# Linear attention beside a gated FFN on one core: Q and K weights loaded in row chunks among the first x tiles, and another order of phase 1

## The chip, the cores and the metric

The kernel runs on one core of a Trainium2 chip. A core has a matrix engine (TensorE, PE in the profile), three engines for elementwise work (VectorE or DVE, ScalarE or ACT, GpSimd or POOL), a queue engine (SyncE or SP) and 16 DMA engines. Each engine works through its own list of instructions in order; engines wait for each other and for transfers by semaphores. Data lies in SBUF (128 partitions); TensorE writes to PSUM, which has eight banks of 128 x 512 float32. The metric is device time in microseconds.

## The reference

With x of 2048 rows and 512 columns in bfloat16, the result is x plus a linear attention block plus a gated FFN, both on the layer norm of x. The attention has 32 heads of 16 columns.

```python
xn = _layernorm(x, axis=-1)
# attention
q, k, v = ...            # xn @ wqkv, split and put by heads
phi = lambda t: jnp.where(t > 0, t + 1, jnp.exp(t)) + 1e-6
pq, pk = phi(q), phi(k)
kv = jnp.einsum("bhsd,bhse->bhde", pk, v)
z = jnp.einsum("bhsd->bhd", pk)
num = jnp.einsum("bhqd,bhde->bhqe", pq, kv)
den = jnp.einsum("bhqd,bhd->bhq", pq, z)[..., None] + 1e-6
A = (num / den) @ wo
# FFN
B = (_silu(xn @ w_gate) * (xn @ w_up)) @ w_down
out = x + A + B
```

## The kernel before

The 2048 rows are 16 tiles of 128; the 512 columns are four chunks of 128. The program lists every operation with the tiles it reads and writes (`K.add`), and a small planner puts in the semaphore waits that these need. The order in the list is the order on each engine.

Phase 1 takes each row tile t through: statistics of the layer norm (step S, VectorE: bn_stats and bn_aggr), 1/std by a logarithm and an exponent on ACT (R), the normalised tile xn on VectorE (L), POOL (P) or ACT (N, then A), its transpose by a DMA (D, issued by SP) or on TensorE (W, X, with the eviction w, Z), the projections K and Q (K and k, Q and q: two halves of four matmuls of 512 columns), phi on them (exponent on ACT: x for K, y for Q; minimum on POOL: m, n; sum on VectorE: s, u), and G += xn^T pk, four matmuls into banks 0 to 3 over all tiles (step G). K and Q go round banks 4 to 7: `nextbank()` hands them out in turn, and the sum (s, u) frees them. For five tiles Q is copied off its bank by ACT (z), and its sum is made much later from the copy.

Tiles 0 and 1 are special (`CENTRED`): they are transposed on TensorE after the mean alone is taken off (a, b: two column halves on VectorE; c, d: two transposes each; e on ACT and f on VectorE evict them into `xcT`), and the 1/std enters later, as the scale of the exponent; r, o, j, J make the other factors. Tile 1's mean comes from ACT (M), and C centres it.

The order of phase 1 is written out by hand: the text given to `run()` is a list of steps, a letter and a tile each. SP issues the x loads ahead of it (tiles 0, 1, 3 to 15; ACT issues half of tile 0 and tile 2), then the transposing loads D in the order of the text, and behind them the weights of gate and up, V, wo and down. Wq and Wk are four loads of two row chunks each, two on ACT and two on SP, behind x tile 3. `keep_busy` runs matmuls on a constant into bank 7: NWARM of them at the start, and step F two of 256 columns.

Phase 2 has 56 groups gu(j) of four gate and four up matmuls, two banks each (4, 5 for even j, 6, 7 for odd j), with a SiLU on ACT and a product on VectorE (`hop`). From the G of phase 1 come GT (evicted ahead of j = 0) and kv (in j = 2). The sum of pk over all rows is made in two halves: POOL adds tiles 0 to 9 behind its last step of phase 1 (`z_add(0, i)`), VectorE the others between products; `z_bf` (behind hop(6)) adds the halves, and the denominators come from it by way of DMAs from j = 13 on. Row tiles of the result are made from j = 19 on.

Lines that matter: 207 to 227 the loads, 251 the warm-up, 257 to 302 statistics and centring, 354 to 368 transposes and evictions, 381 to 397 banks and projections, 399 to 432 phi, 470 to 499 the steps and their order, 500 to 509 the later weights, 515 to 537 gate and up, 558 z_bf, 637 on the order of phase 2.

## Time and profile before

| | us |
|---|---|
| median of 3 runs | 213.74 (212.69 to 214.31) |
| span of the profiled execution | 211.5 |
| busy: TensorE | 207.4 |
| busy: VectorE | 133.9 |
| busy: ACT | 69.6 |
| busy: POOL | 65.4 |

The span runs from the first to the last instruction of one profiled execution; the time of a run also has what lies around it. Busy time is the union of an engine's instructions, so TensorE at 98% says that it nearly always has something in hand, not that this is all necessary work: the warm-up counts too. The page cuts the span into 40 slices of 5.3 us, and each digit is a tenth of busy time:

```profile
PE   8999999999999999999999999999999999999996
...
DVE  3999988964765369746546585756647754625122
ACT  5698977406363333031221322130123131220000
POOL 3697877899500162202102021202202210000000
DMA  5933442399921201111011011011010111011101
```

Phase 1 is the first nine slices: there VectorE, ACT and POOL are nearly as busy as TensorE. Behind it they have room. DMA is busy at the start (x, Wq, Wk) and around the end of phase 1 (the other weights). The rest of a page has the chain of waits that ended last, groups of instructions with their mean duration, and transfers from issue to landing.

### The profile page before, as it was taken

The page shows a single profiled execution, that of the slowest core. Times are in us where ns is not written, and L with a number is a line of the kernel's source. Part 1 is how long each engine was busy: PE and PEld are TensorE (multiplying, and loading weights), DVE is VectorE, ACT ScalarE, POOL GpSimd, SP SyncE. Part 2 cuts the span into 40 slices and gives each one's busy share as a digit, 9 for nine tenths or more (in the row PEclk, how much of TensorE's full clock was granted, in tenths as well). Part 3 has the DMA queues.
Part 4 walks back from the last instruction along what each step waited for, and adds up shares of the span by engine and source line. Part 5 has one row for each costly group of instructions (what it writes and reads, how often), then busy time and mean ns, then how long its engine had stood idle before and what let it go on. Part 6 is the DMA issues. An engine that isn't in the chain of part 4 may idle for free.

```text
span 211.5 us, 2716 instructions
## 1 busy us (share of the span) xinstructions
PE 207.4 (98%) x991; PEld 96.2 (45%) x1010; DVE 133.9 (63%) x228; ACT 69.6 (33%) x144; POOL 65.4 (31%) x89
## 2 busy tenths in 40 slices
PE   8999999999999999999999999999999999999996
PEld 3344444444544444444444444444444444444455
DVE  3999988964765369746546585756647754625122
ACT  5698977406363333031221322130123131220000
POOL 3697877899500162202102021202202210000000
DMA  5933442399921201111011011011010111011101
GB/s 179 355 86 76 79 95 56 88 385 371 356 68 25 53 0 25 25 50 50 2 50 25 25 29 50 0 50 25 28 50 0 26 50 50 4 49 25 50 25 53
DMA packets 28285, 16.30 MB, mean 77 GB/s; under 512 B 18032, under 2 KB 28144, under 8 KB 28272
## 3 DMA queue, kind: packets, MB, share of 16 engines
q1 hardware_dynamic: 27440, 15.41, 26.1%
q10 hardware_dynamic: 832, 0.72, 1.0%
q8 instruction: 8, 0.13, 0.3%
q14 instruction: 5, 0.04, 0.1%
HBM read 9.96 MB, written 2.10 MB: 57 GB/s over the span
## 4 chain that ended last, share of the span: by engine, by line
PE 94%; DMA 2%; DVE 1%; issue 1%; SPq 1%; POOL 0%; ACT 0%; DVEq 0%
PE pb L522 45%; PE pb L620 23%; PE pb L391 12%; PE pb L616 7%; PE pb L440 6%; DMA wqkv<-in_A_wqkv_dram 2%; SPq L181 1%; PE pb L547 0%; PE pb L610 0%; DVE pq L430 0%; DVE hT L535 0%; POOL ef L419 0%; ACT ef L412 0%; PE pb L358 0%; DVE xn L328 0%
## 5 line engine op out<-in xcount | busy, mean ns | idle before, releaser
L530 ACT ACTIVATE sil<-pb 128x512 bf16<-128x512 f32 x56 | 33.3, 597 | 102.4 <-PE pb L522 98.7
L535 DVE TENSOR_TENSOR hT<-pb,sil 128x512 bf16<-128x512 f32 x56 | 38.2, 689 | 42.8 <-PE pb L522 39.9
L522 PE MATMUL pb<-xnT,wg 128*128 128x512 bf16 x224 | 57.8, 379 | 0.4
L522 PE MATMUL pb<-xnT,wu 128*128 128x512 bf16 x215 | 56.0, 379 | 0.2
L580 POOL TENSOR_TENSOR pz<-pq,zbc 128x512 f32<-128x512 bf16 x16 | 22.2, 1392 | 96.8 <-DVE den L587 79.5
L620 PE MATMUL pb<-wd,hT 128*128 128x512 bf16 (+2 forms) x247 | 50.8, 355 | 0.2
L620 PEld LDWEIGHTS pb<-wd,hT 128*128 128x128 bf16 x252 | 23.6, 98 | 24.9
L522 PEld LDWEIGHTS pb<-xnT,wu 128*128 128x128 bf16 x224 | 21.8, 98 | 26.4 <-DVE hT L535 1.4
L522 PEld LDWEIGHTS pb<-xnT,wg 128*128 128x128 bf16 x224 | 21.9, 98 | 25.8
L626 DVE TENSOR_TENSOR out_sb<-pb,x_sb 128x512 bf16<-128x512 f32 (+2 forms) x18 | 11.4, 633 | 23.1 <-PE pb L620 22.1
L391 PE MATMUL pb<-wqkv,xnT 128*128 128x512 bf16 x110 | 25.1, 379 | 0.2
L599 DVE TENSOR_TENSOR pq<-pq,rden 128x512 bf16<-128x512 bf16 x16 | 20.6, 1290 | 0.6
L419 POOL TENSOR_SCALAR ef<-ef 128x512 bf16<-128x512 bf16 x25 | 15.6, 622 | 5.7 <-ACT ef L412 5.4
L391 PEld LDWEIGHTS pb<-wqkv,xnT 128*128 128x128 bf16 x112 | 10.9, 98 | 13.3 <-DVE pk L430 0.4
L616 PE MATMUL pb<-M,pk 128*128 128x512 bf16 (+2 forms) x71 | 16.7, 355 | 0.2
L412 ACT ACTIVATE ef<-pb 128x512 bf16<-128x512 f32 x25 | 14.8, 593 | 3.9 <-PE pb L391 3.9
L258 DVE BATCH_NORM_STATS2 stats<-x_sb 128x6 f32<-128x512 bf16 x16 | 10.8, 678 | 3.2 <-DMA x_sb<-in_A_x_dram 3.2
L440 PE MATMUL pb<-pk,xn 128*128 128x512 bf16 x55 | 12.5, 379 | 0.1
L587 DVE TENSOR_REDUCE den<-pz 128x32 f32<-128x512 f32 x16 | 10.8, 675 | 0.0
L616 PEld LDWEIGHTS pb<-M,pk 128*128 128x128 bf16 x72 | 6.8, 98 | 7.4
L463 POOL TENSOR_TENSOR zacc<-zacc,pk 128x512 f32<-128x512 f32 x8 | 9.9, 1242 | 0.6
L430 DVE SCALAR_TENSOR_TENSOR pk<-pb,ef 128x512 bf16<-128x512 f32 x14 | 9.5, 683 | 0.6 <-POOL ef L419 0.3
(74 smaller groups left out, 111.1 us busy)
## 6 DMA issues: line engine op xcount, KB each, us to landing
out_dram<-out_sb SPq DMA_DIRECT2D x15, 128.0 KB, 1.9
x_sb<-in_A_x_dram SPq DMA_DIRECT2D x14, 128.0 KB, 4.6
wg<-in_B_w_gate_dram SPq DMA_DIRECT2D x2, 896.0 KB, 8.2
wu<-in_B_w_up_dram SPq DMA_DIRECT2D x2, 896.0 KB, 9.6
wd<-in_B_w_down_dram SPq DMA_DIRECT2D x2, 896.0 KB, 13.0
wqkv<-in_A_wqkv_dram ACTq DMA_DIRECT2D x2, 256.0 KB, 4.7
wqkv<-in_A_wqkv_dram SPq DMA_DIRECT2D x2, 256.0 KB, 5.4
wqkv<-in_A_wqkv_dram SPq DMA_DIRECT2D x1, 512.0 KB, 8.9
```

Of the source, the lines that this page charges most:

```text
L391: K.add("pe", [(lambda e, c=c: e.matmul(banks[b][:, :], src[:, c, t * P:(t + 1) * P], wqkv[:, c, col:col + D], start=(c == 0), stop=(c == ...
L412: K.add("act", lambda e: e.activation(buf, banks[b][:, :], ACT.Exp), r=[B(b)], w=[bkey])
L419: K.add("pool", lambda e: e.tensor_scalar(out=buf, in0=buf, scalar1=top, scalar2=0.0, op0=ALU.min, op1=ALU.max), r=[bkey] + tkeys, w=[bkey])
L440: K.add("pe", [(lambda e, c=c: e.matmul(banks[c][:, :], src[:, t, c * P:(c + 1) * P], pk[:, t, :], start=first, stop=last)) for c in range ...
L522: fns.append(lambda e, c=c, b=b, w_=w_: e.matmul(banks[b][:, :], w_[:, c, fc * P:(fc + 1) * P], xnT[:, c, C * 512:(C + 1) * 512], start=(c ...
L530: K.add("act", lambda e: e.activation(sil[:, j % 2, :], banks[gb(j)][:, :], ACT.Silu), r=[B(gb(j))], w=[("sil", j % 2)])
L535: K.add("dve", lambda e: e.tensor_tensor(out=hT[:, C % 2, fc, :], in0=banks[gb(j) + 1][:, :], in1=sil[:, j % 2, :], op=ALU.mult), r=[B(gb( ...
L580: K.add("pool", lambda e: e.tensor_tensor(out=pz[:, t % 2, :].rearrange("q (g p) -> q g p", g=NG), in0=pq[:, t, :].rearrange("q (g p) -> q ...
L599: K.add("dve", lambda e: e.tensor_tensor(out=heads(pq[:, t, :]), in0=heads(pq[:, t, :]), in1=rden[:, i, :][:, :, None].broadcast_to([P, NH ...
L616: fns = [(lambda e, g=g: e.matmul(banks[bank][:, 0:hi - lo], pk[:, t, g * P:(g + 1) * P], M[:, g, lo:hi], start=(g == 0), stop=False)) for ...
L620: fns = [(lambda e, fc=fc: e.matmul(banks[bank][:, 0:hi - lo], hT[:, C % 2, fc, jj * P:(jj + 1) * P], wd[:, fc, lo:hi], start=False, stop= ...
L626: K.add("dve", lambda e: e.tensor_tensor(out=out_sb[:, t % 2, lo:hi], in0=banks[bank][:, 0:hi - lo], in1=x_sb[:, t, lo:hi], op=ALU.add), r ...
```

## The change

Wq and Wk are loaded in four row chunks of 128 rows each, K on SP and Q on ACT, and x tiles 0, 1 and 2 in column halves on both queues among them; ACT also loads tile 3. The other x tiles become steps of the order (l), issued by SP between the transposing loads. The statistics of tile 0 are taken from two halves. Tile 1 is centred like tile 0 (a, b from VectorE's statistics, with transposes c, d and evictions g, h of its own); M, C, N and A are no longer used. A projection step names its chunks: `K0:0` is chunk 0 of K of tile 0, `Q2:01` two chunks, `K3` all four; a bank's first and last chunk set start and stop. K and Q of tile 2 use banks 0 and 1, and phi gets two more buffers for them. The order of phase 1 is new. Of the warm-up, seven matmuls of 512 columns and two of 256 stay, all at the start.

```diff
-SPLIT = (0, 1, 2, 3)
-NWARM = 8
+NC = len(CENTRED)
+NH2 = 3
+LOWBANK = {(1, 2): 0, (0, 2): 1}
+NWARM = 7
...
-        ef = sb("ef", [P, 4, D], bf)
+        ef = sb("ef", [P, 6, D], bf)
...
-        def wpart(eng, i, h):
-            load(eng, ("wqkv", i, h), wqkv[:, 2 * h:2 * h + 2, i * D:(i + 1) * D],
-                 A_wqkv[2 * h * P:(2 * h + 2) * P, i * D:(i + 1) * D].rearrange("(c p) f -> p c f", p=P))
-
-        xhalf("sp", 0, 0)
-        xhalf("act", 0, 1)
-        xload("sp", 1)
-        xload("act", 2)
-        xload("sp", 3)
-        wpart("act", 1, 0)
-        wpart("sp", 1, 1)
-        wpart("act", 0, 0)
-        wpart("sp", 0, 1)
-        for t in range(4, 16):
-            xload("sp", t)
+        def wchunk(eng, i, c):
+            load(eng, ("wqk", i, c), wqkv[:, c, i * D:(i + 1) * D], A_wqkv[c * P:(c + 1) * P, i * D:(i + 1) * D])
+
+        for eng, h in (("sp", 0), ("act", 1)):
+            xhalf(eng, 0, h)
+            wchunk(eng, 1 - h, 0)
+            xhalf(eng, 1, h)
+            wchunk(eng, 1 - h, 1)
+            xhalf(eng, 2, h)
+            wchunk(eng, 1 - h, 2)
+            wchunk(eng, 1 - h, 3)
+            if h:
+                xload(eng, 3)
...


         def xk(t):
-            return [("x", 0, 0), ("x", 0, 1)] if t == 0 else [("x", t)]
+            return [("x", t, 0), ("x", t, 1)] if t < NH2 else [("x", t)]

         def bn1(t):
             K.add("dve", lambda e: e.bn_stats(stats[:, t, :], x_sb[:, t, :]), r=xk(t), w=[("st", t)])

+        def bnhalf(h):
+            K.add("dve", lambda e: e.bn_stats(stats[:, h * NT, :], x_sb[:, 0, h * H:(h + 1) * H]), r=[("x", 0, h)], w=[("st", h * NT)])
+
         def bn2(t):
             K.add("dve", lambda e: e.bn_aggr(mv[:, t, :], stats[:, t, :]), r=[("st", t)], w=[("mv", t)])
+
+        def stat0():
+            bnhalf(0)
+            bnhalf(1)
+            K.add("dve", lambda e: e.bn_aggr(mv[:, 0, :], stats[:, 0::NT, :]), r=[("st", 0), ("st", NT)], w=[("mv", 0)])

         def rs(t):
             sl = slice(t, t + 1)
...

         ring = [0]
         at = {}
+        begun = {}

         def nextbank():
             ring[0] += 1
             return 4 + (ring[0] - 1) % 4

-        def proj(col, i, t, halves=(0, 1)):
-            if 0 in halves:
-                at[i, t] = nextbank()
-            b = at[i, t]
+        def proj(i, t, cs):
+            if (i, t) not in at:
+                at[i, t] = LOWBANK[i, t] if (i, t) in LOWBANK else nextbank()
+                begun[i, t] = 0
+            b, col = at[i, t], i * D
             src = xcT if t in CENTRED else xnT
-            for h in halves:
-                K.add("pe", [(lambda e, c=c: e.matmul(
-                    banks[b][:, :], src[:, c, t * P:(t + 1) * P], wqkv[:, c, col:col + D],
-                    start=(c == 0), stop=(c == NDC - 1))) for c in (2 * h, 2 * h + 1)],
-                    r=([("xcT", t, h)] if t in CENTRED else xkeys(t)) + [("wqkv", i, h)], w=[B(b)])
-
-        def rest(t):
-            return (1,) if t in SPLIT else (0, 1)
+            fns = []
+            for c in cs:
+                first, last = begun[i, t] == 0, begun[i, t] == NDC - 1
+                begun[i, t] += 1
+                fns.append(lambda e, c=c, first=first, last=last: e.matmul(
+                    banks[b][:, :], src[:, c, t * P:(t + 1) * P], wqkv[:, c, col:col + D], start=first, stop=last))
+            keys = sorted({("xcT", t, c // 2) for c in cs}) if t in CENTRED else xkeys(t)
+            K.add("pe", fns, r=keys + [("wqk", i, c) for c in cs], w=[B(b)])
+
+        def efslot(b):
+            return b - 4 if b >= 4 else b + 4

         def phi_keep(t):
             b, slot = at[0, t], later[t]
...
                   r=[fkey, ("pk", t)], w=[key])

         def stat(t):
+            if t == 0:
+                stat0()
+                return
             bn1(t)
             bn2(t)

...
-            "c": lambda t: transp(t, 0, 0, 2), "d": lambda t: transp(t, 1, 2, 4),
-            "e": lambda t: evac(t, 0, "act", 0, 2), "g": lambda t: evac(t, 0, "dve", 0, 2),
-            "h": lambda t: evac(t, 1, "act", 2, 4), "f": lambda t: evac(t, 1, "dve", 2, 4),
+            "c": lambda t: transp(t, 2 * t, 0, 2), "d": lambda t: transp(t, 2 * t + 1, 2, 4),
+            "e": lambda t: evac(t, 2 * t, "act", 0, 2), "g": lambda t: evac(t, 2 * t, "dve", 0, 2),
+            "h": lambda t: evac(t, 2 * t + 1, "act", 2, 4), "f": lambda t: evac(t, 2 * t + 1, "dve", 2, 4),
-            "K": lambda t: proj(D, 1, t, (0,)), "k": lambda t: proj(D, 1, t, rest(t)), "x": lambda t: phi_exp(1, t), "m": lambda t: phi_min(1, t), "s": lambda t: phi_sum(1, t),
-            "Q": lambda t: proj(0, 0, t, (0,)), "q": lambda t: proj(0, 0, t, rest(t)), "y": lambda t: phi_exp(0, t), "z": phi_keep, "n": lambda t: phi_min(0, t), "u": lambda t: phi_sum(0, t), "G": gacc, "F": lambda t: keep_busy(t, 256),
+            "l": lambda t: xload("sp", t), "K": lambda t, cs=range(NDC): proj(1, t, cs), "x": lambda t: phi_exp(1, t), "m": lambda t: phi_min(1, t), "s": lambda t: phi_sum(1, t),
+            "Q": lambda t, cs=range(NDC): proj(0, t, cs), "y": lambda t: phi_exp(0, t), "z": phi_keep, "n": lambda t: phi_min(0, t), "u": lambda t: phi_sum(0, t), "G": gacc, "F": lambda t: keep_busy(t, 256),
+            words = [(w[0], int(w[1:].split(":")[0]), [int(c) for c in w.split(":")[1]] if ":" in w else None)
+                     for w in text.split()]
+            late = {t for k, t, _ in words if k == "z"}
+            later.update({t: i for i, t in enumerate(t for k, t, _ in words if k == "u" and t in late)})
+            for k, t, cs in words:
+                steps[k](t) if cs is None else steps[k](t, cs)
...
         run("""
...
+            F1 l4 l8 F1 S0 l12 b0 d0 R0 a0 c0 e0 r0 Q0:0 S1 a1 c1 Q0:1 J0 b1 d1 R1 r1 o1 l11 f0 S2 h1 o0 g1 K0:0 K0:1
+            l13 K0:2 l14 Q0:2 Q1:0 Q1:1 R2 K0:3 K1:0 L2 W2 Q0:3 K1:1 K1:2 K1:3 l9 x0 Q1:2 m0 z0 S3 R3 w2 y0 S4 P3 R4
+            P4 Q2:01 K2:01 K2:23 x2 m2 S8 X3 x1 l10 Z3 s0 Q2:23 s2 D4 m1 s1 Q1:3 K3 l6 J1 S10 y2 z2 R8 x3 S12 S14 P8
+            m3 z1 Q3 L0 l15 z3 y1 R12 P12 G2 G0 y3 s3 R14 P14 G1 S9 K4 x4 Q4 l7 m4 s4 G3 y4 S13 R10 S6 D8 n4 u4 n3 Q8
+            y8 z8 D12 P10 l5 K8 D14 x8 G4 R9 L9 R6 K12 x12 m8 s8 S7 D10 D9 R13 Q12 P6 Q14 y14 m12 L13 n1 s12 y12 K14
+            x14 G8 G12 S15 n14 u14 Q9 R7 n12 u12 K9 D13 m14 L1 K10 L7 y9 x9 m9 n9 D6 s14 x10 K6 G14 S5 S11 R5 s9 G9
+            x6 R11 u9 K13 m10 s10 L5 R15 L15 D7 K7 x13 m6 s6 Q13 D1 m13 Q10 x7 D15 m7 L11 s13 y13 G10 n13 y10 Q7 y7
+            s7 Q15 u13 D11 n10 u10 y15 K15 D5 n15 x15 n7 G13 u7 Q5 m15 y5 s15 u15 u1 n5 u5 G6 u3 K11 n2 u2 x11 m11
+            s11 n0 K5 x5 m5 s5 Q11 u0 G15 y11 n11 G7 n8 u8 Q6 y6 u11 n6 D0 G11 G5 u6
```

## The prediction

> **What bounds the kernel now.** I read the page first, then the chain of waits, then TensorE's timeline of the first 10 us. The page: lines of its first and fourth part.
>
> ```profile
> span 211.5 us, 2716 instructions
> ...
> PE 207.4 (98%) x991; PEld 96.2 (45%) x1010; DVE 133.9 (63%) x228; ACT 69.6 (33%) x144; POOL 65.4 (31%) x89
> ...
> PE 94%; DMA 2%; DVE 1%; issue 1%; SPq 1%; POOL 0%; ACT 0%; DVEq 0%
> ```
>
> TensorE is busy for all but 4.1 us. So the change can win only what TensorE loses outside its necessary work. The chain (start, us, what) says where that is:
>
> ```profile
> 2.19 5.18 DMA wqkv<-in_A_wqkv_dram
> 7.38 0.05 issue
> 7.42 0.60 PE pb L391 x2
> 8.03 0.22 PE pb L358 x4
> 8.25 0.86 PE pb L391 x4
> ...
> 40.04 4.53 PE pb L440 x21
> ```
>
> The only transfer on it is the second half of the K weights, which lands at 7.37 and lets go two matmuls at 7.42. Behind that the chain is TensorE itself. A 512-column matmul costs 4.53/21 = 0.216 us, a transpose 0.22/4 = 0.055. TensorE's timeline (start, length, what) has the beginning:
>
> ```profile
> 0.84 3.57 PE L248 MATMUL pb<-const-bfloat16-1.0 128*128 128x512 bf16 x8 [0.84 <-PEq L704]
> 4.29 0.61 PE L358 MATMUL pb<-ident,hT 128*128 128x128 bf16 x4
> 4.70 0.63 PE L248 MATMUL pb<-const-bfloat16-1.0 128*128 128x256 bf16 x2
> 5.12 0.63 PE L358 MATMUL pb<-ident,hT 128*128 128x128 bf16 x4
> 5.66 1.60 PE L391 MATMUL pb<-wqkv,hT 128*128 128x512 bf16 x4
> ...
> 48.51 1.03 PE L522 MATMUL pb<-xnT,wg 128*128 128x512 bf16 x4
> ```
>
> Phase 1 is 128 projection and 64 G matmuls and 16 transposes: 192 x 0.216 + 16 x 0.055 = 42.3 us. Phase 2 starts at 48.51, so TensorE has lost 48.5 - 42.3 = 6.2 us: the **head**. The same count at the first G matmul (11.39: 20 matmuls and 16 transposes, 5.2 us) gives 6.2 too. So nothing is lost between 11.4 and 48.5, and a new order of phase 1 can gain nothing there; it can only lose. The change is about these 6.2 us, of which 3.0 pass before x tile 0 has landed (VectorE's first statistics start at 3.00).
>
> **The change, part by part.**
>
> *Warm-up.* Eight matmuls of 512 columns and a later pair of 256 become seven and two, all ahead. They run at (3.57 - 0.63)/7 = 0.42 us, half of the later pace. 7 x 0.42 + 2 x 0.21 = 3.4 us as before (8 x 0.42): the first transposes come at 4.3 again. Nothing fills TensorE between them and the first projection now.
>
> *Loads.* Per queue 64 KB halves of x 0, 1, 2 alternate with 128 KB weight chunks (K on SP, Q on ACT). An issue costs 0.95/2 = 0.48 on SP and 0.49 on ACT. ACT's own instructions stand behind eight issues, until 0.83 + 8 x 0.47 = 4.6, where they stood behind four (to 2.7). Before, ACT began its first exponent step at 4.46, so R0 and the eviction e0 come some 0.2 late, e0 at 5.1 (4.88). The row of stretches shows 27, 274, 263, 293, 321, 356 and 378 GB/s for the microseconds from 1 to 8, so 0.30, 0.56, 0.86, 1.18, 1.53 and 1.91 MB by 3, 4, 5, 6, 7, 8. The landing follows the bytes with a lag: x3 (the first 0.52 MB, 3.85) was used at 5.19, lag 1.3; x0 0.6; the K half of the chain 1.8. With lags of 0.6 to 1.3 in the new order: x1 (0.52 MB) at 4.5 to 5.2, chunks 2 (1.18 MB) at 6.6 to 7.3, chunks 3 (1.44 MB) at 7.35 to 8.05, x3 (1.7 MB) at 8.1 to 8.7. Later x loads move behind transposing transfers on SP (x6, x15, x7 behind tile 4's, which waits for POOL's xn; x5 behind tile 12's): tile 6's statistics come near 20, its load near 13, which hides it.
>
> *Tile 0's statistics in halves.* No row has 256 elements; the 512 form takes 0.69. Two halves cost between 0.69 and 1.37 together, with the first startable 0.15 earlier. The two centring halves of 0.28 start 0.20 apart, so starts overlap: I take no change.
>
> *Tile 1.* Its mean on ACT (0.63 + 0.19) and centring (0.35, done at 4.94) give way to statistics on VectorE: x1 at 4.7, 0.69 + 0.18 + two halves, transposes at 6.0 instead of 5.12.
>
> *K, Q of tiles 0, 1 by chunks.* No matmul is added; only the wait is finer. Walking TensorE's new order on these rows: transposes of tile 0 at 4.3 to 4.8; e0 until 5.43; Q0 chunk 0 at 5.5 (slow, 0.42); tile 1's transposes and Q0 chunk 1 to 6.5; K0 chunks 0 to 2 and Q0 chunk 2 to 7.4; Q1 chunks 0, 1 (behind VectorE's S2 and g1, 7.3) to 7.85; K0 chunk 3 and K1 chunk 0 to 8.3; then tile 2's transposes, whose xn stands behind S2, R2, L2 (8.3). Done by then: 10 matmuls and 8 transposes, 2.6 us; head 5.7. With the lag of 1.3, S1 starts at 5.2, all behind it slides 0.45, and the head is 6.15. So this part gives between -0.5 and 0; between the rows of lag I take the middle of the upper half, **-0.3**.
>
> *New order of phase 1.* Each engine's queue is summed from its rows (exponent 0.48 start to start, statistics 0.79, sum 0.58, minimum 0.58, POOL normalise 1.05) against TensorE's pace of 0.86 for four matmuls. ACT loses M1 and two normalisations, POOL gets two. The thinnest places: Q2's copy off bank 1 (ACT, 13.3) before the first G at 13.5; K4's bank (Q1 off at 15.9, wanted 16.1); tile 8's transposed x (17.8, wanted 18.7). All hold with 0.1 to 0.9, and a slip costs itself once. **0**, up to +1.
>
> *End of phase 1.* TensorE's last work is now Q6, G11, G5, where it was G7 after Q6 long done. VectorE still has s11 s5 u0 u8 u11 u6 to do, and phase 2's first two groups want the banks of Q11 and Q6, which u11 and u6 free. At 0.58 to 0.69 each, u11 is done at 47.2 and u6 at 48.2, wanted at 48.1 and 48.9. The same sums from the copied tiles took up to 1.75 beside POOL (two in 2.77 at 43.10): then up to +0.6. I take 0. Behind it POOL's z sums slide: n6 is last on POOL, at 47.5 instead of 41.4, and its steps of the z sums behind n6 end at 47.5 + (55.9 - 41.4) = 62.0, against z_bf's start at 63.2 - 0.3.
>
> ```profile
> 45.40 10.48 POOL L463 TENSOR_TENSOR zacc<-zacc,pk 128x512 f32<-128x512 f32 x8
> ```
>
> ```profile
> 63.23 0.68 DVE L559 TENSOR_TENSOR zb<-zacc 128x512 bf16<-128x512 f32 x1
> ```
>
> The cover of 7.3 us shrinks to about 0.9: free while it holds. Gate and up weights follow the last transposing load on SP: tile 11's xn is done near 33, three issues of 1.27 on, 37; they started at 39.36. Free.
>
> Sum: 211.5 - 0.3 = 211.2 of span. The median of the runs is 213.74, so 2.2 us lie around the span; that stays: **213.4**.
>
> **The rivals.**
>
> *No earlier start.* The finer pieces land when the coarse ones did, since the transfers are bound together: from 2 us on the DMA share is 0.85 to 1.09. The Trainium skill (DMA: Bandwidth & Descriptors, "Issuing engines are not separate DMA queues") says that starting on two engines saves only issue time; the trace agrees, as the rate stays at 263 to 378 GB/s with both queues full. With slips of the order of 0 to 1 the time is 213.7 to 214.7.
>
> *TensorE's slow pace lasts longer.* The granted clock is 1.00 in every row, yet matmuls run at 0.42 until between 5.7 and 7.4 and at 0.216 after. Until then TensorE had been busy without a gap over 0.2 us. The new order leaves it idle from 4.8 to 5.5 and in small holes up to 6. If this puts the switch off by as long as the warm-up is, 3.4 us, 3.4 us of work takes twice its time: +1.7, less the holes that it fills, +1.5: 214.9; twice so long, 216.6. Against it: the idle 0.7 us is a fifth of that stretch. The Trainium skill (TensorE: Matmul & The Clock Gate, Part 1) describes such a gate, with a free-running window of 3.4 us in which TensorE must be busy; an added idle piece in it speaks against this change, and by it the delay would be whole windows.
>
> *A late POOL holds VectorE.* z_bf waits for POOL's z sums, and behind it VectorE holds the products of gate and up, which free the banks. POOL has 0.9 in hand; the next product after z_bf has 0.8 more. Past 1.7 each microsecond of lateness is one of TensorE. A queue of phase 1 that trails TensorE by 4 us gives 211.2 + 2.3 + 2.2 = 215.7 and more, slower by over 1%. For it: VectorE was busy 37.7 of the 40 us from 5 to 45, and minimum, sum and free bank follow each other with gaps of 0.2. Against it: the sums hold at each place.
>
> *Faster by over 1%* needs a head of 4.1. The first projection can't start before 5.5 by x0's statistics, so only the noise of the runs (212.69 to 214.31) gives it.
>
> **How the numbers follow.** Forecast (span shorter by 0.1 to 0.6) 0.50; no earlier start 0.22; slow pace by one stretch 0.10, by two 0.03; late POOL or a trailing queue 0.12; faster by over 1% 0.03. One per cent is 2.1 us, about what a measurement can tell from no change. Slower: 0.03 + 0.12 and nothing of the rest, less a share of the trailing cases that stay under 2.1 us (0.01): 0.14. Same: 0.83. Faster: 0.03. The range runs from the forecast's -0.6 with the runs' own spread (212.5) to the slow pace of one stretch with some slips (215.3); both ends leave out the last rivals.
>
> **What would show it.** The step is right if the first gate matmul starts between 47.9 and 48.4 at an unchanged matmul pace, if no DMA stands at the head of the chain from 7.4 on, and if the first full-pace projection comes before 7. It is wrong if warm-up pace is seen past 8, if TensorE waits for a bank or for z_bf, or if VectorE's S1 starts after 5.2.

## The result, and the profile after

The changed kernel takes 215.57 us (median of five runs, 215.0 to 216.26) against 213.74 before: a ratio of 1.0094, interval 1.0065 to 1.0124. The forecast was 213.4. The profiled execution of the changed kernel has a span of 215.0, 3.5 more than before. That is more than the 1.8 between the medians, because the execution profiled here was the longest of its five (216.26) and the one profiled before the shortest of its own (212.69). Lines of the changed kernel's page, its first, second and fourth part:

```profile
PE 209.3 (97%) x1009; PEld 96.0 (45%) x1009; DVE 135.7 (63%) x230; ACT 68.1 (32%) x141; POOL 67.5 (31%) x91
...
PEclk9699999999999999999999999999999999999999
...
PE 92%; DMA 2%; DVE 2%; POOL 1%; ACT 0%; ACTq 0%; issue 0%; DVEq 0%
```

TensorE is idle for 5.7 us in place of 4.1, and VectorE and POOL have a larger share of the chain (1% and 0% before). The second slice of the granted clock (the share of TensorE's full clock that the chip lets it have) shows a 6, where every slice was full before. TensorE's timeline (start, length, what; in brackets the idle time ahead and its releaser) has the places:

```profile
4.30 0.48 PE L366 MATMUL pb<-ident,hT 128*128 128x128 bf16 x4 [0.17 <-DVE hT L298]
5.57 0.39 PE L404 MATMUL pb<-wqkv,hT 128*128 128x512 bf16 x1 [0.78 <-ACT hT L374]
...
6.75 0.39 PE L404 MATMUL pb<-wqkv,hT 128*128 128x512 bf16 x1 [0.59 <-DMA wqkv<-in_A_wqkv_dram]
...
7.08 3.57 PE L404 MATMUL pb<-wqkv,hT 128*128 128x512 bf16 x8
...
51.67 1.02 PE L540 MATMUL pb<-xnT,wg 128*128 128x512 bf16 x4 [1.03 <-DVE pq L443]
```

Phase 2 starts at 51.67, where it started at 48.51: 3.16 of the 3.5 us are lost ahead of it. Three things are to be seen. Q0's second chunk is waited for until 6.75. The eight matmuls from 7.08 take 3.57, 0.42 or more from one start to the next in place of 0.216, though TensorE no longer waits for anything. And 1.03 us pass ahead of phase 2 until VectorE has made a sum. The stretches of 3.4 us around 7.1 (length; busy time and instructions of PE, PEld, DVE, ACT, POOL; granted clock; DMA share; GB/s) show that the second of these is the clock:

```profile
3.70:7.10 3.40, 1.86 (x14) 0.77 (x13) 2.25 (x8) 1.71 (x11) 1.33 (x4) 1.00 0.93 260
7.10:10.50 3.40, 3.40 (x12) 1.12 (x10) 2.34 (x6) 1.11 (x4) 0.48 (x3) 0.50 1.03 352
```

In the first TensorE is busy 1.86 of 3.4 us; in the next it is always busy and granted half its clock. Half a clock for 3.4 us costs 1.7 us of work, and 1.7 of a span of 215 is the 0.992 that this execution has as its mean granted clock. VectorE's timeline at the end of phase 1:

```profile
48.14 0.69 DVE L443 SCALAR_TENSOR_TENSOR pk<-pb,ef 128x512 bf16<-128x512 f32 x1 [0.56 <-POOL ef L432]
48.75 1.05 DVE L443 SCALAR_TENSOR_TENSOR pq<-hT,flo,pq 128x512 bf16<-128x512 f32 x1
49.73 1.09 DVE L443 SCALAR_TENSOR_TENSOR pq<-hT,pq 128x512 bf16<-128x512 f32 x1
50.74 1.27 DVE L443 SCALAR_TENSOR_TENSOR pq<-pb,ef 128x512 bf16<-128x512 f32 x2
```

The two sums whose input is hT are u0 and u8, made from copies, and nobody waits for them. Behind them stands u11 (the first of the last pair), which frees bank 4 for phase 2.

Some runs of the changed kernel have a mean granted clock of 0.992 and some of 1.000, so a median of few runs moves with how many there are of each. Over these five runs and four later ones: 215.0 to 215.7 (five runs at 1.000, mean 215.45) and 216.26 to 217.64 (four at 0.992, mean 216.93).

### The profile page after: what moved, and what is told of

It reads as the page before. It is cut to its first block, busy times and chain, and to the rows that moved or that the text cites. A ratio compares the mean times of both kernels' runs of the same rounds, so it can differ in the third digit from the quotient of the medians.

```text
span 215.0 us, 2744 instructions
## 1 busy us (share of the span) xinstructions
PE 209.3 (97%) x1009; PEld 96.0 (45%) x1009; DVE 135.7 (63%) x230; ACT 68.1 (32%) x141; POOL 67.5 (31%) x91
## 4 chain that ended last, share of the span: by engine, by line
PE 92%; DMA 2%; DVE 2%; POOL 1%; ACT 0%; ACTq 0%; issue 0%; DVEq 0%
PE pb L540 45%; PE pb L638 23%; PE pb L404 13%; PE pb L634 6%; PE pb L453 5%; DMA wqkv<-in_A_wqkv_dram 2%; DVE pq L443 1%; POOL ef L432 1%; POOL pq L432 1%; ACTq L183 0%; PE pb L565 0%; PE pb L628 0%; DVE pk L443 0%; DVE hT L553 0%; PE pb L366 0%
## 5 line engine op out<-in xcount | busy, mean ns | idle before, releaser
L540 PE MATMUL pb<-xnT,wu 128*128 128x512 bf16 x224 | 57.8, 379 | 0.1
L638 PE MATMUL pb<-wd,hT 128*128 128x512 bf16 (+2 forms) x252 | 51.4, 355 | 0.0
L404 PE MATMUL pb<-wqkv,xnT 128*128 128x512 bf16 x112 | 26.2, 379 | 0.0
L644 DVE TENSOR_TENSOR out_sb<-pb,x_sb 128x512 bf16<-128x512 f32 (+2 forms) x18 | 11.4, 632 | 23.1 <-PE pb L638 23.1
L453 PE MATMUL pb<-pk,xn 128*128 128x512 bf16 x56 | 13.7, 379 | 0.0
L258 DVE BATCH_NORM_STATS2 stats<-x_sb 128x6 f32<-128x512 bf16 x15 | 10.2, 678 | 1.4 <-DMA x_sb<-in_A_x_dram 1.2
L476 POOL TENSOR_TENSOR zacc<-zacc,pk 128x512 f32<-128x512 f32 x8 | 10.6, 1319 | 0.6
```

Source lines behind the costliest of these rows:

```text
L404: fns.append(lambda e, c=c, first=first, last=last: e.matmul(banks[b][:, :], src[:, c, t * P:(t + 1) * P], wqkv[:, c, col:col + D], start= ...
L453: K.add("pe", [(lambda e, c=c: e.matmul(banks[c][:, :], src[:, t, c * P:(c + 1) * P], pk[:, t, :], start=first, stop=last)) for c in range ...
L540: fns.append(lambda e, c=c, b=b, w_=w_: e.matmul(banks[b][:, :], w_[:, c, fc * P:(fc + 1) * P], xnT[:, c, C * 512:(C + 1) * 512], start=(c ...
L638: fns = [(lambda e, fc=fc: e.matmul(banks[bank][:, 0:hi - lo], hT[:, C % 2, fc, jj * P:(jj + 1) * P], wd[:, fc, lo:hi], start=False, stop= ...
```

## The experiments

In the table "filled" means matmuls on constants put into TensorE's idle stretches; the ratio is to the kernel before, run on the same chip in the same job.

| label | kernel | us (median, runs) | before | ratio, 95% interval |
|---|---|---|---|---|
| again | changed kernel, unaltered | 216.9, 4 | 213.03 | 1.0182, 1.0136 to 1.0228 |
| tail | u0, u8 behind u11, u6 | 214.55, 9 | 213.03 | 1.0081, 1.0042 to 1.0119 |
| fill | idle stretches filled, 2 x 3 matmuls | 215.24, 4 | 213.03 | 1.0122, 1.0079 to 1.0165 |
| newloads | new loads, old order of phase 1 | 219.2, 4 | 213.03 | 1.0291, 1.0255 to 1.0326 |
| tail_fill | tail, filled with 3 and 6 | 214.71, 6 | 212.97 | 1.0071, 1.0040 to 1.0101 |
| tail_flat | tail, weights read contiguously | 215.25, 4 | 212.97 | 1.0113, 1.0046 to 1.0180 |
| tail_rows | tail, x 1 and 2 split by rows | 216.2, 4 | 212.97 | 1.0142, 1.0093 to 1.0190 |
| reorder | tail, all first chunks' matmuls first | 216.11, 4 | 212.97 | 1.0146, 1.0111 to 1.0181 |
| b_chunks | before, weights in 128 KB chunks | 213.73, 10 | 213.09 | 1.0033, 0.9995 to 1.0071 |
| b_xhalf | before, x 1 and 2 in halves | 213.41, 10 | 213.09 | 1.0016, 0.9997 to 1.0035 |
| b_cold | before, no warm-up | 213.81, 9 | 213.09 | 1.0046, 1.0020 to 1.0071 |
| tf_xfront | tail_fill, later x loads at the front | 215.11, 4 | 213.09 | 1.0098, 1.0069 to 1.0127 |
| tf_xfirst | tail_fill, x 0 to 2 ahead of the chunks | 214.43, 7 | 213.48 | 1.0053, 1.0029 to 1.0077 |
| b_pair | b_chunks, K on one queue, Q on the other | 213.63, 1 | 213.48 | one run |
| b_mix | b_chunks, x and K chunks in turns | 214.74, 1 | 213.48 | one run |
| tf_shift | tf_xfirst, filled with fewer matmuls | 213.71, 12 | 213.19 | 1.0017, 0.9994 to 1.0040 |

### The end of phase 1

`again` is the changed kernel itself, for the spread of its runs and as the neighbour of the others. `tail` moves two sums:

```diff
-            s11 n0 K5 x5 m5 s5 Q11 u0 G15 y11 n11 G7 n8 u8 Q6 y6 u11 n6 D0 G11 G5 u6
+            s11 n0 K5 x5 m5 s5 Q11 G15 y11 n11 G7 n8 Q6 y6 u11 n6 D0 G11 G5 u6 u0 u8
```

> The changed kernel once more, nothing altered. In its first profile TensorE waited 1.0 us for VectorE's sum u11 between phase 1 and 2, and the granted clock fell to 0.5 from 7.1 to 10.5 us. Theory A (three losses: the end of phase 1 about 1.0, the idle start that lets the clock fall up to 1.7, chunk 1 of K and Q landing at 6.5 to 6.7 instead of 5.3, 0.6): the wait for u11 comes again at 0.8 to 1.2; the drop of the clock need not, since the other runs show a mean clock of 1.000 and spans 0.6 to 1.3 shorter. Rival B (the clock alone makes the kernel slow): without the drop the ratio to before is within 0.3% of 1.

> The sums u0 and u8 (read from the copies, 1.05 and 1.09 us beside POOL) go behind u11 and u6. Theory A: the wait of the first gate matmul shrinks from 1.0 to under 0.3 and the time falls by 0.8 to 1.0 us against the changed kernel. Rival: u11 and u6 are then held by POOL's n11 and n6, or the evictions of G behind u0 and u8 come too late for kv, and less than 0.3 us is won.

`again` repeated the wait (1.0 us for u11) and the fall of the clock, from 8 to 11.5. In `tail` the wait is gone; TensorE's timeline goes from the last G to phase 2 without a gap:

```profile
47.68 1.89 PE L453 MATMUL pb<-pk,xn 128*128 128x512 bf16 x8
49.41 1.03 PE L540 MATMUL pb<-xnT,wg 128*128 128x512 bf16 x4
```

Among runs at a clock of 1.000 the median falls from 215.57 (five runs) to 214.36 (seven of `tail`): 1.2, about the 1.0 us of the wait. (The means fall by less, from 215.45 to 214.71, because one of the seven took 216.74 at a full clock; why it did is not known.) So this loss is a steady one, and its cause is shown: two sums that no one waits for, in front of one that frees a bank.

### The clock

`fill` (F3 twice) and `tail_fill` (F3 and F6, with the moved sums as well) put matmuls on constants into the two idle stretches; `b_cold` leaves out the eight warm-up matmuls of the kernel before.

```diff
 # tail_fill
-            ... d0 R0 a0 c0 e0 r0 Q0:0 S1 a1 c1 Q0:1 ...
+            ... d0 R0 a0 c0 F3 e0 r0 Q0:0 S1 a1 c1 F6 Q0:1 ...
```

> Three matmuls of 256 columns on the constant go into each of the two idle stretches of the start (4.8 to 5.6, 6.2 to 6.8). Theory A: TensorE's idle time before 7 us shrinks from 1.5 to about 0.5 us, the granted clock stays at 1.00, and the time falls by 0 to 1.7 us against the changed kernel, 0.8 in the median if about half of its runs lose the clock. Rival: the clock falls anyway or never mattered in the timed runs: within 0.3 us of the changed kernel.

> tail with three matmuls of 256 columns on the constant behind tile 0's transposes and six behind tile 1's first two. Theory A (a stretch of 3.4 us with TensorE idle for more than about half of it makes the clock fall, price 1.5 us): no run with a mean clock under 1.000 (tail had 2 of 9), median 0.2 to 0.6 us under tail's 214.55. Rival B (the drop comes at random and the idle time is not its cause): runs at 0.992 as often as before, median that of tail or later by the added work (up to 0.5).

> The kernel before without its eight warm-up matmuls on constants (no work of the result is left out). It prices TensorE's slow pace by itself. Theory: TensorE starts at 4.3 us in place of 0.84, so the slow pace lasts 3.4 us longer into the useful work, from about 7.2 to about 10.6; the twelve or so projection matmuls of that stretch take 0.4 us each in place of 0.2, and the first accumulation of G starts 0.8 to 1.7 us later than 11.39: 213.8 to 214.7. Rival: TensorE waits for loads there anyway, the slow pace is hidden by those waits, and the time stays within 0.4 of the kernel before.

The mean granted clock was 0.992 in four of nine runs of the changed kernel (after and `again`), in two of nine of `tail` and in one of four of `fill`, whose second stretch gets three matmuls only. It was 0.992 in none of the 25 runs of `tail_fill`, `tf_xfirst` and `tf_shift`, which fill more, and in three of the 72 runs of the kernel before in the jobs of these experiments; what made those three fall is not known. The stretches of `tail_fill`:

```profile
3.70:7.10 3.40, 2.92 (x23) 1.65 (x22) 2.37 (x9) 1.71 (x11) 1.34 (x4) 1.00 0.88 249
7.10:10.50 3.40, 3.34 (x17) 1.16 (x15) 2.16 (x7) 2.15 (x5) 1.13 (x4) 1.00 1.04 357
```

TensorE is busy 2.92 of 3.4 us ahead of 7.1 (3.27 in the kernel before, 1.86 in the changed one), and the clock stays. Filling cures the fall: the idle stretches are its cause in the changed kernel.

The traces also suggest why only some executions fall. Their records of the clock come in stretches of 3.41 us or multiples of it, and the first record begins at another time in each trace: at 3.71 in the changed kernel's first profile and at 4.65 in `again`, the same program. The falls go with how busy TensorE is in the first 3.41 us from there. It was busy for 29% in `newloads`, 41% in `tail_rows`, 44% in `tail_flat`, 52% in `again` and 55% in the first profile, and in these five the clock halved for the next stretch (in `newloads` for the next two). It was busy for 56% in `tail`, 63% in `b_pair` and 80% and more in the five others with records from the start, and none of these fell. That is twelve profiles, no run set the share on purpose, and the limit is known no better than this.

The price of a fall is the difference of the two groups of runs above, 1.5 us. It is not all that spreads the runs: `tail` took 215.27 and 216.24 in its two runs at 0.992, and 216.74 in one at 1.000. The Trainium skill (TensorE: Matmul & The Clock Gate, Part 1) gives the half clock after an idle window of about 3.4 us. The length agrees with the 3.4 us of the trace. But TensorE was not idle in the window ahead: it was busy for 55% of it (1.86 of 3.4).

`b_cold` started its first projections at the slow pace and kept it until about 9.5 in the profiled execution, with a granted clock of 1.00 in all its rows (its trace has no record of the clock, and the view prints 1.00 where there is none):

```profile
5.90 1.87 PE L390 MATMUL pb<-wqkv,hT 128*128 128x512 bf16 x4
8.28 1.03 PE L390 MATMUL pb<-wqkv,hT 128*128 128x512 bf16 x2 [0.52 <-DMA wqkv<-in_A_wqkv_dram]
...
13.30 1.03 PE L439 MATMUL pb<-pk,hT 128*128 128x512 bf16 x4
```

Its first G comes 1.9 late (11.39 before). That execution took 214.78; the median, 213.81, is only 0.7 above the kernel before. The other runs lie 0.2 to 2.1 above it, one 4.1. So the slow pace has its price in the kernel before too, but in most runs at the low end of what was expected. It may be that part of it passes while TensorE would wait for weights anyway; no run shows how much.

### Why the chunks land late

In the changed kernel the second K chunk landed at 6.51 and the second Q chunk at 6.70 (the last of 16 DMA engines), with the same 768 KB asked for ahead of or with them as with the first K half before, which landed at 5.53. 15 of the 16 engines had K's chunk in by 4.98; one was 1.5 late. What differs is the rate, in GB/s the last number of a row. Rows of the changed kernel, then of `b_chunks`, from 4 to 6 us:

```profile
4.00:5.00 1.00, 0.61 (x6) 0.23 (x4) 0.86 (x3) 0.29 (x1) 0.28 (x1) 1.00 1.09 238
5.00:6.00 1.00, 0.43 (x3) 0.21 (x3) 0.93 (x5) 0.94 (x7) 0.12 (x1) 1.00 0.62 196
```

```profile
4.00:5.00 1.00, 0.96 (x7) 0.34 (x6) 0.59 (x3) 0.92 (x4) 0.00 (x0) 1.00 1.03 328
5.00:6.00 1.00, 0.40 (x4) 0.23 (x4) 0.96 (x4) 0.74 (x5) 0.54 (x3) 1.00 1.03 328
```

The new loads move 238 and 196 GB/s; the kernel before moved 293 and 321, and `b_chunks` 328 and 328. The trace's records of single packets show a part of the reason: most packets of 1 KB take 0.046 us, but a few, between 4 and 7 us, take 0.3 to 1.6. The kernel before has such packets as well (12 of 0.3 us and more between 1 and 8 us, the longest 0.75). What differs is how much time they take between 4 and 6 us, where 16 engines have 32 us together: packets of over 0.2 us take 6.2 of these in the changed kernel and 2.2 in the kernel before. They are not the whole of it, for in `b_mix`, below, they take 6.7 and the rate is higher (239 and 362). Nine runs looked for the cause. They change, one by one: the order of phase 1 back to the old one (`newloads`); the source of the weights (`tail_flat`: `A_wo` and `B_w_down` in place of K's and Q's columns, rows of 1 KB that follow each other, so that its K and Q are made from other weights than the reference's); halves of x by rows in place of columns (`tail_rows`); the use of the chunks (`reorder`); and, in the kernel before, each part of the new loads alone.

```diff
 # tail_flat
-A_wqkv[c * P:(c + 1) * P, i * D:(i + 1) * D]
+(A_wo if i else B_w_down)[c * P:(c + 1) * P, :]
 # tail_rows, t = 1, 2
-x_sb[:, t, h * H:(h + 1) * H]
+x_sb[h * P // 2:(h + 1) * P // 2, t, :]
 # reorder
-... Q0:0 S1 a1 c1 Q0:1 J0 b1 d1 R1 r1 o1 l11 f0 S2 h1 o0 g1 K0:0 K0:1 ...
+... Q0:0 K0:0 S1 a1 c1 J0 b1 d1 R1 r1 o1 l11 f0 g1 S2 h1 o0 Q1:0 K1:0 Q0:1 K0:1 ...
 # b_chunks
-load(eng, ("wqkv", i, h), wqkv[:, 2 * h:2 * h + 2, i * D:(i + 1) * D], ...)
+for c in (2 * h, 2 * h + 1):
+    load(eng, ("wqk", i, c), wqkv[:, c, i * D:(i + 1) * D], ...)
 # b_xhalf
-xload("sp", 1); xload("act", 2)
+xhalf("sp", 1, 0); xhalf("act", 1, 1); xhalf("sp", 2, 0); xhalf("act", 2, 1)
 # b_pair, on b_chunks
-wpart("act", 1, 0); wpart("sp", 1, 1); wpart("act", 0, 0); wpart("sp", 0, 1)
+for h in (0, 1): wpart("act", 1, h); wpart("sp", 0, h)
 # b_mix, on b_chunks
-xload("sp", 1); xload("act", 2); xload("sp", 3); wpart("act", 1, 0); wpart("sp", 1, 1)
+xload("sp", 1); wchunk("act", 1, 0); wchunk("sp", 1, 2); xload("act", 2); xload("sp", 3)
+wchunk("act", 1, 1); wchunk("sp", 1, 3)
 # tf_xfirst, on tail_fill, each queue
-x0 half, chunk 0, x1 half, chunk 1, x2 half, chunk 2, chunk 3
+x0 half, x1 half, x2 half, chunk 0, chunk 1, chunk 2, chunk 3
```

> The kernel before with only the loads changed: K and Q in row chunks on SP and ACT among halves of x 0, 1, 2, x 3 on ACT, then x 4 to 15 on SP; order of phase 1, statistics, tile 1's centring and warm-up as before. Theory A: K's first half is complete at 6.5 instead of 5.5, so K0 starts near 6.6 and the kernel is 0.5 to 1.0 us slower than before. Rival (the late chunk was an accident of one profiled run): chunks 0 and 1 have landed by 5.5 and the time is within 0.3 us of before.

> tail with K's chunks read from wo and Q's from the first rows of w_down, where a chunk of 128 rows is one piece of 128 KB, instead of wqkv, where 1 KB pieces lie 3 KB apart: other weights, same sizes. Theory A (single packets of the strided rows that take 0.3 to 1.6 us instead of 0.046 hold chunk 1 back): chunk 1 has landed by 5.5 on both queues, Q0's chunk 1 no longer waits (0.8 before), the time falls by 0.5 to 1.0 us against tail. Rival B (chunk 1 is late because the DMA engines are busy with what was issued ahead): chunk 1 still at 6.3 to 7.0, time within 0.3 us of tail.

> tail with x 1 and 2 split between the queues by rows (64 rows of 1 KB each) instead of by columns (128 rows of 512 bytes). Theory C (the 512-byte pieces slow the transfers between 4 and 6 us): chunk 1 lands 0.4 us or more earlier, 0.3 to 0.6 us won against tail. Rival: within 0.3 us of tail.

> tail with the start put into the order of landing: chunk 0 of K0 and Q0, then chunk 0 of K1 and Q1, before any chunk 1; tile 1's eviction g ahead of tile 2's statistics; tile 2's transposes evicted by ACT. Theory A (TensorE's losses are the wait for chunk 1 and the clock): TensorE has two to four more matmuls done by 7.0, the head at the first G is 5.8 to 6.3 (7.0 in tail), the time falls by 0.6 to 1.0 us against tail and comes within 0.5 us of before. Rival (the new order only moves the wait to tile 2's statistics, which need x 2 at 7.1 to 7.4): under 0.3 us.

> The kernel before, with one thing of the change alone: its four 256 KB loads of Q and K weights become eight of 128 KB (one row chunk each), on the same queues and in the same places, and the projections still wait for pairs of chunks. Theory A (small loads land late by themselves: the changed kernel's second chunks landed at 6.5 to 6.7 us with the same 768 KB ahead as in the kernel before, whose first K half landed at 5.53): the second K chunk lands at 6.3 us or later, the projection that waits for it starts that much later, and the time is 0.5 to 1.2 above the kernel before. Rival B (the lateness comes from what is mixed: x halves between the weights, both queues reading the same x tile): the second K chunk lands by 5.8 and the time is within 0.5 of the kernel before. Either way four more issues of about 0.4 us on each of the two queues' engines; the end of phase 1 is untouched, so a wait there would refute both.

> The kernel before, with the other thing of the change alone: x tiles 1 and 2 are loaded in two column halves, one on each queue, in place of one whole tile on each queue; weights as before. Theory A of the run beside it (loads of 128 KB for the weights are the cause): the first K half lands at 5.5 to 5.8, the second at 7.4 to 7.7, and the time is within 0.4 of the kernel before. Rival B (x in halves is the cause): the first K half lands at 6.3 or later, the second at 8 or later, and the time is 0.5 to 1.2 above the kernel before. If neither of the two runs lands late, the cause is the interleaving of x and weights, or the order in which bytes of one queue pass the other's.

> The kernel before with chunked weights (213.73), where the two queues read K and Q at once as in the change: the four K chunks follow each other on ScalarE's queue, the four Q chunks on SyncE's, all x tiles ahead of them whole as before. One look, for the rate of the DMA engines. Rival P (pairing): below 260 GB/s in the microseconds from 4.5 to 6.5 and chunks landing with single engines 1 us late. Theory M (taking turns): 290 or more, as in the kernel with chunked weights alone (328 and 328). The time goes up a little either way, since the last K chunk now lands with the last Q chunk: 213.2 to 214.8.

> The kernel before with chunked weights (213.73), with whole x tiles and K chunks taking turns on each queue (x0 half, x1, K chunk 2, x3, K chunk 3 on the one; x0 half, K chunk 0, x2, K chunk 1 on the other; Q after them). One look, for the rate of the DMA engines. Theory M (taking turns): 128 to 289 GB/s from 4 to 6 us, with single engines 1 to 2 us late on a chunk. Rival P (pairing): 290 or more. If both this and the run beside it keep the rate, only the three together (halves, turns, pairs) make it fall, and the cause stays open.

> The run with the late sums moved and the idle stretches filled (214.71), with the first loads of each queue in another order: the halves of x tiles 0, 1 and 2 first, then the four weight chunks (K's on the one queue, Q's on the other as before), then x tile 3. In all ten profiles of the changed load order the DMA engines moved 128 to 289 GB/s from 4 to 6 us, in all four of the old order (chunked weights and halved x among them) 293 to 346. Theory M (x pieces and weight chunks taking turns on a queue cause it): the rate from 4 to 6 us is 290 or more, the second chunks of K and Q (384 + 512 KB) land by 6.0 to 6.4, the third and fourth half a microsecond earlier than 7.8 and 8.6, and the time is 0.3 to 0.8 lower, 213.9 to 214.4. Rival P (the two queues reading K and Q chunks at once causes it): the rate falls below 260 again, the second chunks land at 6.7 or later, and the time is 214.7 to 215.5, since the first chunks also come 0.8 later.

The rates, read from the same rows of one profile of each (GB/s in the microsecond that begins at 3, 4, 5), and the bytes moved by 6 us as their sum from 1 us on. A second profile of the changed kernel (`again`) has 320, 199 and 201, so differences of 40 say little:

| kernel | 3 | 4 | 5 | MB by 6 us |
|---|---|---|---|---|
| before | 263 | 293 | 321 | 1.18 |
| b_chunks | 342 | 328 | 328 | 1.19 |
| b_xhalf | 171 | 329 | 346 | 1.12 |
| b_pair | 368 | 329 | 283 | 1.16 |
| b_mix | 263 | 239 | 362 | 1.08 |
| after | 315 | 238 | 196 | 1.01 |
| newloads | 279 | 253 | 245 | 1.00 |
| tail_flat | 336 | 223 | 218 | 0.97 |
| tail_rows | 237 | 185 | 289 | 0.95 |
| reorder | 270 | 175 | 206 | 0.93 |
| tf_xfirst | 154 | 227 | 353 | 1.01 |

Neither the small loads nor the halves of x alone bring the dip (`b_chunks`, `b_xhalf`; both within 0.4% of the kernel before), nor do strided rows (`tail_flat` has it with contiguous ones: its second chunk was used at 7.5), nor columns of 512 bytes (`tail_rows`). The last three runs were to tell two theories apart. Pairs of K and Q are not it: `b_pair` has 329 and 283, a little under the 290 that was set for this and far above the changed kernel's 196. Turns of x and weights seem to have a part: `b_mix` has 239 in one microsecond and is 0.11 MB behind `b_chunks` at 6 us, where the changed kernel is 0.18 behind. But `tf_xfirst`, without turns, has the dip too, one microsecond earlier (154 and 227), where its x halves end and the chunks begin; `b_xhalf` has a short one at the same place (171). So no single part that was tried makes it in full, `b_pair` and `b_mix` rest on one run each, and the cause of the low rate and of the long packets stays open. What is shown is that each kernel of the table with the new pieces together has the dip, and that its place can be moved: in `tf_xfirst` the rate is back at 353 by 5 us, the chunks are all used without a wait, and phase 2 starts at 49.85 in place of `tail_fill`'s 50.26. The Trainium skill (DMA: Bandwidth & Descriptors, "Latency and other measured facts") gives 0.2 us for an access of the memory on average and 2 us under high load. The packets here take 0.046 to 1.6 us, and no run shows that it is the memory that the long ones wait for.

Two of these runs missed for another reason. `newloads` was meant to price the loads alone, but the old order has VectorE work on x tile 3 ahead of the copy that TensorE waits for, and the new loads bring x3 last (9.34 in the changed kernel):

```profile
10.83 1.46 PE L395 MATMUL pb<-wqkv,hT 128*128 128x512 bf16 x3 [3.79 <-DVE hT L372]
```

With 3.79 us idle its clock fell too, in three of four runs for two stretches (0.984). So the new order of phase 1 isn't free to choose; the new loads need it. `reorder` got x1 late (5.06 and 5.26, in place of 4.33 and 4.56) and kept the slow pace of the start for longer: 12 matmuls from 7.56 take 3.60, which is 2.6 at 0.216, with the granted clock at 1.00; then it waited 0.7 for an eviction that had been given to ScalarE.

### The wait for tile 8

Once tail and clock were mended, `tail_fill` showed a new wait, 0.70 us at 20.9 for the transposing load of tile 8. Its engines landed from 18.81 on, one at 20.85. `tf_xfront` takes away the x loads that stand ahead of it on SP (all twelve are issued behind the weights); `tf_shift` makes the filling matmuls, in `tf_xfirst`, four of 512 columns (1 and 3) in place of nine of 256.

```diff
 # tf_xfront
-F1 l4 l8 F1 S0 l12 ... l11 ... l13 ... l14 ... l9 ... l10 ... l6 ... l15 ... l7 ... l5 ...
+F1 l4 l8 l12 l11 l13 l14 l9 l10 l6 l15 l7 l5 F1 S0 ...
 # tf_shift
-... a0 c0 F3 e0 r0 Q0:0 S1 a1 c1 F6 Q0:1 ...
+... a0 c0 V1 e0 r0 Q0:0 S1 a1 c1 V3 Q0:1 ...     # V: keep_busy(t, 512)
```

> The run with the late sums moved and the idle stretches filled (214.71), with the twelve x loads of tiles 4 to 15 issued one after the other behind the weights, before the first transposing load, in place of being spread among the steps. Theory: in that run the transposing load of tile 8 was issued behind three x loads of 1.5 us on the SyncE queue and one of 16 engines landed it at 20.85, for which TensorE waited 0.7 us at the projection of tile 8; with the x loads ahead it lands about 2.5 us after its issue, the wait goes, and the time is 0.4 to 0.8 lower, 213.9 to 214.3, still not below the kernel before. Rival: the twelve loads now share the DMA engines with the last two weight chunks and x tile 3, which land 0.5 us later or more, the head grows by as much, and the time is 214.6 to 215.3.

> The run with x first (214.43), with its nine filling matmuls of 256 columns made into four of 512, so that TensorE's program is five matmuls and five weight loads shorter before the end of phase 1. Theory: in the three runs that fill the idle stretches the transposing load of tile 8 has one of 16 engines late by 2 us, since a 16 KB fetch of instructions runs on that engine (18.42 to 19.36 there); the fetch comes when TensorE has passed a certain instruction, so with ten fewer it starts 0.8 to 1.2 later, at 19.2 to 19.6, after tile 8 has landed at 18.5; TensorE's wait of 0.75 goes, or is under 0.3, the first gate matmul starts at 49.1 to 49.4 in place of 49.85, and the time is 0.4 to 0.8 lower: 213.6 to 214.0. Rival (the load is late by itself, as POOL hands over tile 8 late): the wait stays at 0.6 to 0.8 wherever the fetch falls, and the time stays at 214.2 to 214.7. If the fetch doesn't move, nothing is told.

`tf_xfront` refuted the first idea: the load of tile 8 was issued at 16.62 and its last engine landed at 20.96, a wait of 0.73. The records of transfers then showed a fetch of 16 KB of instructions on one DMA engine at 18.81, 18.66 and 18.42 in `tail_fill`, `tf_xfront` and `tf_xfirst`, about 1 us long. The records don't name the engine, but the late one landed tile 8 some 1.0 us after the fetch ended, in all three. The fetch comes at about the same place in TensorE's program: 80 to 85 records of its matmuls lie ahead of it in every kernel of the new order, whether none, four, six or nine of them are filling ones. (`b_cold` doesn't fit so well: with eight matmuls fewer than the kernel before, it has 85 ahead of the fetch in place of 91.) In `tf_shift` the fetch began at 19.45, tile 8 landed at 18.76, and the wait is gone. `fill`, with six filling matmuls, has the same: 19.47 and 18.70. The same matmuls in `tf_xfirst`, then in `tf_shift`:

```profile
20.48 1.90 PE L404 MATMUL pb<-wqkv,xnT 128*128 128x512 bf16 x8 [0.75 <-DMA xnT<-xn]
```

```profile
19.84 1.89 PE L404 MATMUL pb<-wqkv,xnT 128*128 128x512 bf16 x8
...
49.19 1.03 PE L540 MATMUL pb<-xnT,wg 128*128 128x512 bf16 x4
```

Phase 2 starts at 49.19 in place of 49.85, and the time is 213.71, as the theory had it. In the changed kernel as given, the fetch falls at 21.55 and ends while the load of tile 12 is under way (4.1 us from issue to landing); TensorE doesn't wait for that one.

With all four mended (the late sums, the clock, the order of the loads, the fetch), the changed kernel is at 1.0017 (0.9994 to 1.0040): no difference that can be told from the kernel before, and no version beat it.

## Why the prediction was wrong

*The bound was read rightly.* Nothing was lost before between 11.4 and 48.5, and the new order could only lose there. It can be said more sharply now. Of the head of 6.2 us, 5.66 - 8 x 0.055 = 5.2 lie ahead of the first projection, 1.60 - 4 x 0.216 = 0.7 are the slow pace of the first four, and 0.16 is the wait for weights. Four matmuls at full pace show 1.03 (48.51) where 4 x 0.216 is 0.86, so 0.17 of the 0.7 is the last one running out, and the wait costs 0.33 in all. Finer weights could win that, and perhaps some of the slow pace; they could not start the first projection, which came at 5.57, as forecast (5.5), when ScalarE had evicted tile 0.

*Loads: the step that failed first.* The list of landings named x1, chunks 2, chunks 3 and x3, and left out chunk 1 and x2. Chunk 1 was taken as in time for "Q0 chunk 1 to 6.5"; it came at 6.51 and 6.70, and Q0 chunk 1 ran at 6.75. VectorE stood still for 0.89 until x2 came (6.89 and 7.08), ahead of the eviction that Q1 chunk 0 waits for. The forecast took the bytes of the old order's rows for the new one, 0.86 MB by 5 us and 1.18 by 6; the new loads had moved 0.81 and 1.01. x1 came early in its range (4.33 and 4.56); behind the dip all came later than the late end: chunks 2 at 7.61 and 7.82, chunks 3 at 8.36 and 8.58, x3 at 9.34 in place of 8.7. The -0.3 for chunks became a loss of about 0.9 (`tail`: phase 2 at 49.41 with a full clock and no wait at its end; 0.81 of idle time there is the wait for Q0 chunk 1). Not all of it is shown to be the loads: with all chunks in time (`tf_xfirst`) phase 2 comes 0.41 earlier than in `tail_fill`, and the rest was not taken apart.

*Slow pace: the right danger and price, by another path, with too small a chance.* The rival had idle pieces put off the end of the slow pace. Here the slow pace ended in time (the first projection, at 5.57, took 0.39 us; in `fill`, still slow then, it took 0.61), and the idle pieces made the clock fall after that. Both cost one stretch at half pace, so that the price fits is in part luck: +1.5 was named, and a fall costs 1.5. It was given 0.10 for one stretch and comes in four runs of nine. The argument against it, that 0.7 us idle is a fifth of the stretch, counted one gap only. With the gaps of 0.17, 0.78 and 0.59 and the short work between, TensorE was busy 55% of the stretch. A slow pace that lasts longer, as the rival had it, is seen in `reorder`.

*End of phase 1: the term of 0, "up to +0.6", was 1.03.* The forecast saw both parts, u0 and u8 ahead of u11 and sums up to 1.75 beside POOL, and took the cheap end. u11 was put at 47.2 done and phase 2 at 48.1; the sums took 1.05 and 1.09 in place of 0.58 to 0.69, s5 waited 0.56 for POOL, and `tail`, where s5 waits as long (0.57) and TensorE not at all, shows that the place of u0 and u8 in the queue is all of it.

*New order: 0, and it held,* but for the thin place that was named, tile 8's transposed x: it is the next limit as soon as the others are mended, by a fetch that no list of the kernel shows.

*POOL and the z sums.* POOL's part ended at 64.6, not at 62.0. z_bf was late by itself in the changed kernel (66.39), so nothing waited; in `tail` and `tf_shift` it waited 0.2. The cover is used up, as the forecast feared, and no loss from it is seen.

*The sum.* The forecast put 2.2 us around the span, but took the median of the runs against the span of the shortest: that execution took 212.69 with a span of 211.5, so 1.2 lie around it (1.26 in the changed kernel's). This moves the sum's two parts and not the difference that was forecast. The last instruction came 0.33 later than phase 2's delay accounts for. In the changed kernel an 8 KB fetch of instructions runs at 213.60, beside the last store, and before it came at 211.59, after the end. All 18 profiles agree: from phase 2's start to the last matmul's end it is 161.2 us in each, and from there to the end 1.82 to 1.86 in the three where this fetch comes after the end (the kernel before, `b_xhalf`, `b_cold`) and 2.07 to 2.29 in the other fifteen. No run was made to move this fetch alone.

The rival "no earlier start", 213.7 to 214.7 with slips of 0 to 1, is what the kernel does without the wait at the end and the fall of the clock; 215.57, the median, is a run at a full clock: that rival with the wait on top. The runs above 216 have both. Two of the forecast's signs of being wrong came: the pace of the warm-up past 8 us, and a wait for a bank.

## What to carry to other kernels

Before work is made finer, count how much of the lost time the coarse wait holds: here it was 0.3 us of 6.2. When loads are rearranged, list the landing of every piece that something waits for, and don't carry a rate over from another order of loads. At a change of phase, put ahead what frees a buffer and behind what nobody awaits; and where TensorE has several short gaps close together, add them up over a window of 3.4 us; matmuls on constants can fill them, if what they move behind them (here the fetch that met tile 8) is looked at too.

## What the hardware showed

- The granted clock fell to half for 3.4 us after a first stretch of 3.41 us in which TensorE was busy for 29 to 55% (five profiles), and did not after one with 56% or more (seven). Where that stretch begins differs between executions of one program (3.71 and 4.65), which may be why four runs of nine fell and not all; with the gaps filled (86% in `tail_fill`) none of 25 did. The slow pace at the start of a kernel isn't seen in that column: in `b_cold` it reads 1.00 while 512 columns take 0.4 to 0.5 us, since the trace has no record of the clock there.
- Single packets of 1 KB took 0.3 to 1.6 us, where most take 0.046, in the old order of loads (up to 0.75) and in the new; and a transfer over 16 engines is as late as the worst of them (15 by 4.98, the last at 6.51).
- Instructions are fetched by DMA, 16 KB in about 1 us, at about the same place in the program, and a load under way at that time had one of its 16 engines 2 us late in three kernels. Five matmuls fewer ahead of the fetch moved it by 1.03 us, and phase 2 began 0.66 earlier.
